# Signs and low halves of the converted weights on GpSimd in a chain of attention and two expert layers

## The chip, the cores and the metric

One core of one Trainium2 chip runs the whole program in one launch. The metric is the device time of one execution in microseconds; the median over the runs is given. An execution under the profiler gives the trace from which all rows come.

## The reference

Three stages follow one another:

```python
qn = q / (norm(q, axis=1) + 1e-6); kn = k / (norm(k, axis=1) + 1e-6)   # B, N, C = 2, 6016, 256
a = softmax(kn.transpose(0, 2, 1) @ qn / tau)      # 256 x 256 per batch
x = (v @ a).reshape(12032, 256)
h = x @ w_in;  x = (h - tanh(h)) @ w_out           # d_ff 2048
out = (sigmoid(x @ w_gate) * (x @ w_val)) @ w_out2 # d_ff 1536
```

The five weight matrices (w_in, w_out, w_gate, w_val, w_out2) are float64 arrays. They reach the kernel as pairs of 32-bit words and are turned into float32 on the core.

## The kernel before

**Tiling.** The tokens are cut into 24 blocks of 496 or 512 columns, 12 per batch, with the channels on the 128 partitions. Before the blocks the start-up loads q and k of batch 0 in chunks (`load_raw`), multiplies them on TensorE (`boot_s`, L570), squares them on ScalarE (L578) and sums the squares on VectorE into `accb` (L581). The 256x256 softmax (`s_softmax`) follows, and `aw_chunk` multiplies its result into w_in, so that v needs only one product in place of two.

**Steps.** Then one loop over T runs; a step of it handles one slice f of 128 of the 2048 hidden columns of a block: `emit_H` (TensorE, L332 and L334) makes h of slice T, `emit_E` (ScalarE L342 to L346, VectorE L347 to L350) makes h - tanh(h) of slice T - 1, `emit_gs` splits slice T - 2 into a high and a low half (ScalarE L355, VectorE L356), and `emit_X` (L378 to L381) multiplies it. `emit_GV`, `emit_S`, `emit_ps` and `emit_O` do the same for the gated layer, a block behind. Most products are made of three: high by high, high by low and low by high halves of the operands in the format fp32r, of which ScalarE writes the high half as a rounded copy and VectorE the low half as the difference.

**Converting a weight.** `conv` is a generator that runs once for each of 34 tiles of 128x512 elements: 8 of w_in, 8 of w_out, 18 of the gate, value and second output weights. It loads the word pairs (L125) into `st`. ScalarE scales the high words, read as float32, by 2^-112 into `bt` (L135): that puts the exponent right. A second ScalarE instruction (L136) overwrites the upper 16 bits of the high word by a half-precision zero that carries the sign, VectorE shifts the upper three bits of the low word into the lower 16 bits (L138), and a last VectorE instruction shifts `bt` left by three and ors that word in (L143). For the 18 tiles of the gated layer a further step makes the high half (L149) and the low half (L150). `split_w1` does the same for the 8 tiles of w_out (L184, L187).

**Order.** The schedule is written out by hand; each engine works through its own instructions in program order. In `at(step, ...)` a background generator is given a step at which it begins; the list `running` then advances each generator by one `yield None` per step T, after `emit_S` and before `emit_H`. `whole` passes over the `yield 1`, so that the whole conversion (L135 to L143) falls into one step. In start-up the generators `tail` are advanced piece by piece between the pieces of the softmax. The steps GV0 say when a pair of gate and value slices of block 0 is first multiplied; a conversion begins at least three steps before (`late`). The buffers of `st` are 4 in start-up (`boot4`) and 3 later (`v4`), those of `bt` 4 (`cv`). GpSimd holds only the constants, one fill of `accb` and the 46 sums of squares of batch 1 (L688), from 366 us on.

Of the kernel before, what the change touches and what calls it, by code (L numbers as in the profile page):

```python
# [8 lines left out]
F32 = mybir.dt.float32  # L9
F32R = mybir.dt.float32r  # L10
BF16 = mybir.dt.bfloat16
U32 = mybir.dt.uint32
U16 = mybir.dt.uint16
F16 = mybir.dt.float16
AF = mybir.ActivationFunctionType
ALU = mybir.AluOpType
AX = mybir.AxisListType
# [10 lines left out]
def kernel(  # L28
# [13 lines left out]
    nc = tc.nc  # L42
# [18 lines left out]
    rest, i = N - WB * nb, nb // 2  # L61
    assert 0 <= rest <= nb * (TB - WB)
    while rest:
        widths[i] += QB
        rest -= QB
        i = (i + 1) % nb
    blocks = []
    for b in range(B):
        t = 0
# [23 lines left out]
    def cv(name, shape=(P, 512)):  # L93
        return cv_p.tile(list(shape), F32, tag="cv", name=name)
# [22 lines left out]
    w1_hi = [wp.tile([P, 2, C], F32R, name=f"w1h{i}") for i in range(N1 // 2)]  # L117
    w1_lo = {}
    win_d = dr_p.tile([N1 // 2, P, NK, 2 * P], F32, name="win_d")

    def conv(src, shape, pool, tag, name, w=None, hi=None, lo=None):

        a, m = shape
        st = pool.tile([P, a, 2 * m], U32, tag=tag, name=f"st_{name}")
        nc.sync.dma_start(out=st, in_=src)  # L125
        yield
        words = st.rearrange("p a (m t) -> p a m t", t=2)
        low, high = words[:, :, :, 0], words[:, :, :, 1]
        half = st.bitcast(U16).rearrange("p a (m t) -> p a m t", t=4)
        bt = cv(f"cb_{name}", (P, a, m))  # L130
        bu = bt.bitcast(U32)

        nc.scalar.activation(bt, high.bitcast(F32), AF.Copy, scale=2.0**-112)  # L135
        nc.scalar.activation(half[:, :, :, 3].bitcast(F16), high.bitcast(F32), AF.Copy, scale=2.0**-96)  # L136
        yield 1
        nc.vector.tensor_scalar(half[:, :, :, 2], half[:, :, :, 1], 13, None, ALU.logical_shift_right)  # L138
        yield 1
        yield 1  # L140
        if callable(w):
            w = w()
        nc.vector.scalar_tensor_tensor(  # L143
            out=bu if w is None else w.bitcast(U32), in0=bu, scalar=3, in1=high,
            op0=ALU.logical_shift_left, op1=ALU.bitwise_or
        )
        if w is None:
            yield
            nc.scalar.activation(hi, bt, AF.Copy)  # L149
            nc.vector.tensor_tensor(out=lo, in0=bt, in1=hi.bitcast(F32), op=ALU.subtract)  # L150

    def whole(g):

# [7 lines left out]
    def conv_win(i, pool, tag="st"):  # L161
        src = words(w_in)[:, i * 512:(i + 1) * 512].rearrange("(k p) f -> p k f", p=P)
        yield from conv(src, (NK, 2 * P), pool, tag, f"wi{i}", w=win[i])
# [7 lines left out]
    w1_f = {}  # L171

    def conv_w1(i):
        src = words(w_out)[i * 256:(i + 1) * 256, :].rearrange("(a p) d -> p a d", p=P)

        def home():
            pool, tag = (wp, f"w1l{i - 4}") if i > 3 else (wp2, f"w2{'hl'[i % 2]}{4 + i // 2}")
            w1_f[i] = pool.tile([P, 2, C], F32, tag=tag, name=f"w1f{i}")
            return w1_f[i]

        return conv(src, (2, C), v4_p, "v4", f"w1{i}", w=home)

    def split_w1(i):
        nc.scalar.activation(w1_hi[i], w1_f[i], AF.Copy)  # L184
        yield
        w1_lo[i] = wp.tile([P, 2, C], F32R, tag=f"w1l{i}", name=f"w1l{i}")
        nc.vector.tensor_tensor(out=w1_lo[i], in0=w1_f[i], in1=w1_hi[i].bitcast(F32), op=ALU.subtract)  # L187


    kq = {}  # L190
# [469 lines left out]
    def conv_m2(i, which):  # L660
        if which == 2:
            src = words(w_out2)[i * 256:(i + 1) * 256, :].rearrange("(a p) d -> p a d", p=P)
            for x, nm in ((w2_hi, "w2h"), (w2_lo, "w2l")):
                x[i] = wp2.tile([P, 2, 2 * P], F32R, tag=f"{nm}{i}", name=f"{nm}{i}")
            h, lo = w2_hi[i], w2_lo[i]
        else:
            w = (w_gate, w_val)[which]
            src = words(w)[:, i * 512:(i + 1) * 512].rearrange("(k p) f -> p k f", p=P)
            h, lo = ((wg_hi[i], wg_lo[i]), (wv_hi[i], wv_lo[i]))[which]
        return conv(src, (2, 2 * P), v4_p, "v4", f"m{which}{i}", hi=h, lo=lo)  # L670
# [43 lines left out]
    for i in range(N1 // 2):  # L714
        at({6: 16, 2: 18, 7: 19, 3: 20, 4: 21, 5: 23, 0: 25, 1: 26}[i], split_w1, i)
# [5 lines left out]
    for n in range(3 * N2 // 2):  # L721
        i, w = divmod(n, 3)
# [3 lines left out]
    for j in range(NT):  # L726
        t = 54 + 2 * j
# [121 lines left out]
```

## Time and profile before

| what | value |
|---|---|
| median of 3 runs | 2211.52 us (2211.27 to 2211.89) |
| profiled execution | 2212.01 us, of which the span from first to last instruction 2210.2 us |
| TensorE busy | 2199.5 us |
| VectorE busy | 1772.7 us |
| ScalarE busy | 1602.0 us |
| GpSimd busy | 66.5 us |
| granted TensorE clock | 1.0 throughout |

PE is TensorE, PEld its weight loads, DVE VectorE, ACT ScalarE, POOL GpSimd. A row of the timeline gives start and length in us, the engine, the line of the kernel, and output <- inputs; a bracket at its end gives the idle time before it and what ended that. The length of an instruction is longer than its slot on a full engine, since the next one starts before the recorded end.

### The profile page before, as it was taken

To read this page: it belongs to the slowest core of one execution; us is meant where nothing else is said; L and a number is where in the kernel's file an instruction comes from. 1 tells how busy PE (TensorE), PEld (TensorE's weight loads), DVE (VectorE), ACT (ScalarE), POOL (GpSimd) and SP (SyncE) were. 2 spreads that over 40 slices of the span, in tenths; PEclk is the share of its full clock that TensorE was granted. 3 is DMA by queue.
4 is the path that set the end of the run, shared out by engine and by line. 5 is a ranking of instruction groups with operands and counts; after the bars stand their busy time and mean duration, and the time that the engine had idled before them with its cause. 6 is when DMAs were issued, how large, how long until landed. Compare 5 with 4: busy or idle time off the path is not lost.

```text
span 2210.2 us, 28820 instructions
## 1 busy us (share of the span) xinstructions
PE 2199.5 (100%) x10338; PEld 1944.1 (88%) x10338; DVE 1772.7 (80%) x2723; ACT 1602.0 (72%) x2811; POOL 66.5 (3%) x53
## 2 busy tenths in 40 slices
PE   9999999999999999999999999999999999999999
PEld 8778899898888888888999999999988888888898
DVE  7889877888888888878787787787787877877773
ACT  7988867777777777767677676776776776767763
POOL 0000000111111110000000000000000000000000
PEclk9999999999999999999999999999999999999999
DMA  9742101111111010001000000000000000000000
GB/s 354 241 147 96 38 1 53 34 29 52 35 29 48 27 36 20 1 24 34 19 19 1 19 19 1 19 19 1 19 20 1 19 20 1 20 1 19 10 1 19
DMA packets 54000, 86.54 MB, mean 39 GB/s; under 512 B 4960, under 2 KB 31072, under 8 KB 53856
## 3 DMA queue, kind: packets, MB, share of 16 engines
q1 hardware_dynamic: 53280, 83.91, 11.6%
q8 instruction: 81, 1.33, 0.3%
q10 hardware_dynamic: 576, 0.79, 0.1%
q14 instruction: 63, 0.52, 0.1%
HBM read 69.73 MB, written 14.94 MB: 38 GB/s over the span
## 4 chain that ended last, share of the span: by engine, by line
PE 93%; DVE 3%; ACT 3%; issue 1%; DMA 1%; ACTq 0%; DVEq 0%
PE o L445 16%; PE h L332 14%; PE h L334 7%; PE x L381 7%; PE x L378 7%; PE x L379 7%; PE va L414 5%; PE va L416 5%; PE va L413 5%; PE ga L414 5%; PE ga L413 5%; PE ga L416 5%; PE x L373 2%; PE kqe L517 1%; PE aw L285 1%
## 5 line engine op out<-in xcount | busy, mean ns | idle before, releaser
L347 DVE SCALAR_TENSOR_TENSOR w<-u,h 128x496 f32<-128x496 f32 (+1 forms) x384 | 259.6, 676 | 228.6 <-ACT t L343 227.7
L350 DVE COPY_PREDICATED w<-m,t 128x496 f32<-128x496 uint16 (+1 forms) x384 | 303.9, 792 | 39.9 <-ACT sr L687 0.5
L342 ACT ACTIVATE u<-h 128x496 f32<-128x496 f32 (+1 forms) x384 | 222.7, 580 | 138.8 <-PE h L334 138.3
L345 ACT ACTIVATE s<-u,cb 128x496 f32<-128x496 f32 (+1 forms) x384 | 273.8, 713 | 0.3 <-DVE w L349 0.3
L346 ACT ACTIVATE m<-u,ct 128x496 bf16<-128x496 f32 (+1 forms) x384 | 272.5, 710 | 0.0
L348 DVE TENSOR_TENSOR t<-h,t 128x496 f32<-128x496 f32 (+1 forms) x384 | 258.4, 673 | 0.0
L349 DVE SCALAR_TENSOR_TENSOR w<-s,w 128x496 f32<-128x496 f32 (+1 forms) x384 | 257.6, 671 | 0.0
L332 PE MATMUL h<-vTh,awh 128*128 128x496 f32 (+1 forms) x768 | 232.8, 385 | 0.0
L334 PE MATMUL h<-vTh,awl 128*128 128x496 f32 (+1 forms) x768 | 225.1, 375 | 0.2 <-DVE awl L291 0.2
L332 PE MATMUL h<-vTl,awh 128*128 128x496 f32 (+1 forms) x768 | 225.0, 375 | 0.0
L343 ACT ACTIVATE t<-h 128x496 f32<-128x496 f32 (+1 forms) x384 | 223.1, 581 | 0.0
L414 PE MATMUL va<-x2h,wvl 128*128 128x496 f32 (+1 forms) x552 | 206.9, 375 | 0.0
L414 PE MATMUL ga<-x2h,wgl 128*128 128x496 f32 (+1 forms) x552 | 206.9, 375 | 0.0
L413 PE MATMUL va<-x2h,wvh 128*128 128x496 f32 (+1 forms) x552 | 206.9, 375 | 0.0
L413 PE MATMUL ga<-x2h,wgh 128*128 128x496 f32 (+1 forms) x552 | 206.8, 375 | 0.0
L425 DVE TENSOR_TENSOR sg<-va,sg 128x496 f32<-128x496 f32 (+1 forms) x288 | 192.2, 667 | 18.1 <-PE va L416 18.1
L424 ACT ACTIVATE sg<-ga 128x496 f32<-128x496 f32 (+1 forms) x288 | 168.6, 585 | 11.2 <-PE ga L416 11.1
L416 PE MATMUL ga<-x2l,wgh 128*128 128x496 f32 (+1 forms) x576 | 168.8, 375 | 0.0
L416 PE MATMUL va<-x2l,wvh 128*128 128x496 f32 (+1 forms) x576 | 168.8, 375 | 0.0
L332 PEld LDWEIGHTS h<-vTh,awh 128*128 128x128 f32 x768 | 144.4, 189 | 24.5 <-issue 6.8
L334 PEld LDWEIGHTS h<-vTh,awl 128*128 128x128 f32 x768 | 145.1, 189 | 17.7 <-DVE awl L291 0.6
L332 PEld LDWEIGHTS h<-vTl,awh 128*128 128x128 f32 x768 | 145.1, 189 | 17.2
(358 smaller groups left out, 4425.8 us busy)
## 6 DMA issues: line engine op xcount, KB each, us to landing
v<-in_v_dram SPq DMA_DIRECT2D x16, 496.0 KB, 4.2
out_dram<-ob SPq DMA_DIRECT2D x15, 496.0 KB, 3.0
sr<-in_q_dram SPq DMA_DIRECT2D x47, 128.0 KB, 2.1
sr<-in_k_dram SPq DMA_DIRECT2D x47, 128.0 KB, 2.3
raw<-in_q_dram SPq DMA_DIRECT2D x13, 384.0 KB, 8.1
raw<-in_k_dram SPq DMA_DIRECT2D x12, 384.0 KB, 8.2
st_wi<-in_moe_w_in_dram SPq DMA_DIRECT2D x8, 512.0 KB, 7.0
st_w<-in_moe_w_out_dram SPq DMA_DIRECT2D x8, 512.0 KB, 4.7
```

What stands on the lines that cost most here:

```text
L332: MM(o[:, :n], aw_hi[i][:, kk, fs], turned(p, x[:, kk, :n]), start=x is h and kk == 0, stop=False)
L334: MM(o[:, :n], aw_lo[i][:, kk, fs], turned(p, h[:, kk, :n]), start=False, stop=kk == 1)
L345: nc.scalar.activation(s, u, AF.Square, bias=cb)
L346: nc.scalar.activation(m, u, AF.Relu, bias=ct2)
L347: nc.vector.scalar_tensor_tensor(out=w, in0=u, scalar=C2, in1=hp, op0=ALU.mult, op1=ALU.mult)
L348: nc.vector.tensor_tensor(out=t, in0=hp, in1=t, op=ALU.subtract)
L349: nc.vector.scalar_tensor_tensor(out=w, in0=s, scalar=CG, in1=w, op0=ALU.add, op1=ALU.mult)
L350: nc.vector.copy_predicated(w, m.bitcast(U16), t)
L413: MM(o[:, :n], wht[m // 2][:, d, ms], h[d], start=d == 0, stop=False)
L414: MM(o[:, :n], wlt[m // 2][:, d, ms], h[d], start=False, stop=False)
L416: MM(o[:, :n], wht[m // 2][:, d, ms], lo[d], start=False, stop=d == 1)
L445: MM(ops[p][d][:, :n], w[i][:, a, ds[d]], x, start=m == 0 and w is w2_hi and x is ph, stop=m == N2 - 1 and x is pl)
```

## The change

For each converted tile the second ScalarE instruction is left out. GpSimd compares the high word, read as float32, with zero and multiplies by -2^31; written as a 32-bit integer in place, that is the sign bit alone. VectorE shifts the low word right by 29 and ors the sign in, in place of the shift of 16-bit halves; the last shift and or then takes this word. The low halves of the 18 tiles of the gated layer and of the 8 tiles of w_out are subtracted on GpSimd instead of VectorE.

```diff
@@ conv
-        half = st.bitcast(U16).rearrange("p a (m t) -> p a m t", t=4)
...
         nc.scalar.activation(bt, high.bitcast(F32), AF.Copy, scale=2.0**-112)
-        nc.scalar.activation(half[:, :, :, 3].bitcast(F16), high.bitcast(F32), AF.Copy, scale=2.0**-96)
+        nc.gpsimd.tensor_scalar(high.bitcast(I32), high.bitcast(F32), 0.0, -2.0**31, ALU.is_lt, ALU.mult)
         yield 1
-        nc.vector.tensor_scalar(half[:, :, :, 2], half[:, :, :, 1], 13, None, ALU.logical_shift_right)
         yield 1
+        nc.vector.scalar_tensor_tensor(
+            out=low, in0=low, scalar=29, in1=high, op0=ALU.logical_shift_right, op1=ALU.bitwise_or
+        )
         yield 1
...
         nc.vector.scalar_tensor_tensor(
-            out=bu if w is None else w.bitcast(U32), in0=bu, scalar=3, in1=high,
+            out=bu if w is None else w.bitcast(U32), in0=bu, scalar=3, in1=low,
             op0=ALU.logical_shift_left, op1=ALU.bitwise_or
         )
         if w is None:
             yield
             nc.scalar.activation(hi, bt, AF.Copy)
-            nc.vector.tensor_tensor(out=lo, in0=bt, in1=hi.bitcast(F32), op=ALU.subtract)
+            nc.gpsimd.tensor_tensor(out=lo, in0=bt, in1=hi.bitcast(F32), op=ALU.subtract)
@@ split_w1
-        nc.vector.tensor_tensor(out=w1_lo[i], in0=w1_f[i], in1=w1_hi[i].bitcast(F32), op=ALU.subtract)
+        nc.gpsimd.tensor_tensor(out=w1_lo[i], in0=w1_f[i], in1=w1_hi[i].bitcast(F32), op=ALU.subtract)
```

## Rows read from the trace of the kernel before

**Rows 1.** The page's part 1: busy us, share of the span, instructions, by engine.

```profile
PE 2199.5 (100%) x10338; PEld 1944.1 (88%) x10338; DVE 1772.7 (80%) x2723; ACT 1602.0 (72%) x2811; POOL 66.5 (3%) x53
```

**Rows 2.** Busy time of each engine in stretches (the head row names the columns).

```profile
core 0: us, PE busy (x) PEld busy (x) DVE busy (x) ACT busy (x) POOL busy (x), PEclk, DMA share, GB/s
...
12.00:46.00 34.00, 33.35 (x155) 29.41 (x156) 32.23 (x27) 28.48 (x26) 0.00 (x0) 1.00 1.01 376
...
70.00:200.00 130.00, 130.00 (x536) 101.29 (x535) 115.05 (x182) 115.48 (x184) 0.00 (x0) 1.00 0.49 155
200.00:250.00 50.00, 47.94 (x223) 41.18 (x222) 48.10 (x78) 44.93 (x77) 0.00 (x0) 1.00 0.15 47
250.00:2210.00 1960.00, 1955.48 (x9283) 1745.07 (x9281) 1558.91 (x2400) 1388.30 (x2489) 64.44 (x46) 1.00 0.06 20
```

**Rows 3.** Waits of TensorE: who waited for whom, us, times, longest.

```profile
PE va L414 <- DVE wvl L150: 1.5, 1, 1.5
...
PE x L378 <- ACT g_14h L355: 0.6, 1, 0.6
```

**Rows 4.** Timeline of start-up: start, length (us), engine, line, operation.

```profile
45.11 0.63 ACT L578 ACTIVATE sq<-raw 128x512 f32<-128x512 f32 x1 [0.70 <-DVE accb L581]
...
46.58 1.35 ACT L136 ACTIVATE st_wi<-st_wi 128x512 f16<-128x512 f32 x1
...
47.94 1.28 ACT L637 ACT_TABLE_LOAD   x1
...
49.82 1.06 PE L203 MATMUL n<-ones,sq 128*128 128x64 f32 x8
...
50.97 1.35 ACT L136 ACTIVATE st_wi<-st_wi 128x512 f16<-128x512 f32 x1
...
52.07 0.25 ACT L214 ACTIVATE rn<-n 128x4 f32<-128x4 f32 x1
```

**Rows 5.** Timeline of VectorE in start-up, one converted tile.

```profile
21.80 0.74 DVE L138 TENSOR_SCALAR st_wi<-st_wi 128x512 uint16<-128x512 uint16 x1
22.57 0.69 DVE L143 SCALAR_TENSOR_TENSOR win<-cb_wi,st_wi 128x512 uint32<-128x512 uint32 x1
23.18 1.75 DVE L581 TENSOR_TENSOR accb<-accb,sq 128x1536 f32<-128x1536 f32 x1
```

**Rows 6.** Chain that ended last, 185 to 260 us: start, us, what.

```profile
214.61 1.36 ACT st_m L136
...
239.62 0.61 DVE wvl L150
```

**Rows 7.** GpSimd by line: count, busy us, mean ns, idle before.

```profile
L688 POOL TENSOR_TENSOR acc<-acc,sr 128x512 f32<-128x512 f32 x46 | 64.4, 1401 | 790.9 <-ACT sr L687 790.9
L546 POOL MEMSET accb<- 128x1536 f32 x1 | 1.4, 1383 | 0.0
masks.py:199 POOL TENSOR_SCALAR_AFFINE_SELECT ident<-ident 128x128 f32<-128x128 f32 x1 | 0.3, 294 | 0.0
```

**Rows 8.** Timeline around two adds on GpSimd and VectorE beside them.

```profile
377.65 1.27 POOL L688 TENSOR_TENSOR acc<-acc,sr 128x512 f32<-128x512 f32 x1 [10.26 <-ACT sr L687]
...
377.78 1.72 DVE L350 COPY_PREDICATED w<-m,t 128x496 f32<-128x496 uint16 x1
...
387.90 0.72 DVE L350 COPY_PREDICATED w<-m,t 128x496 f32<-128x496 uint16 x1
...
388.25 1.48 POOL L688 TENSOR_TENSOR acc<-acc,sr 128x512 f32<-128x512 f32 x1 [9.33 <-ACT sr L687]
...
389.31 0.95 DVE L356 TENSOR_TENSOR g_11l<-w,g_11h 128x496 fp32r<-128x496 f32 x1
...
390.18 0.66 DVE L356 TENSOR_TENSOR p_7l<-sg,p_7h 128x496 fp32r<-128x496 f32 x1
```

**Rows 9.** VectorE by line, the removed shift of 18 tiles.

```profile
L138 DVE TENSOR_SCALAR st_m<-st_m 128x512 uint16<-128x512 uint16 x18 | 13.5, 748 | 2.4 <-ACT st_m L136 2.4
```

**Rows 10.** Timeline of ScalarE, the last value weight's high half.

```profile
237.32 0.64 ACT L149 ACTIVATE wvh<-cb_m 128x512 fp32r<-128x512 f32 x1
```

More of the change, by code (lines that the diff above doesn't have):

```diff
@@ L13 @@
 U16 = mybir.dt.uint16
-F16 = mybir.dt.float16
+I32 = mybir.dt.int32
 AF = mybir.ActivationFunctionType
```

## The prediction

> **What bounds the kernel now.** I read the page's busy line first: TensorE is busy 2199.5 us of a span of 2210.2 us [rows 1]. The reader is to see that only 10.7 us are not TensorE's, and that no relief of another engine can give more than its part of these. Next I cut the span by stage [rows 2]: from 250 us to the end, where nothing of the change runs, TensorE works 1955.48 of 1960 us. Delay from before 250 us is therefore not won back, and a gain there stays. From 70 to 200 us TensorE never idles, although VectorE works 115.05 of 130 us beside it. From 200 to 250 us it idles 2.06 us, and there VectorE is full: 48.10 of 50 us. The view of waits names what ends TensorE's idle time [rows 3]: the low half of a value weight (1.5 us, once) and the high half of an activation (0.6, once); most of the others are in start-up, before 63 us. The page's own 2212.01 us of the profiled execution stands 0.5 us above the median of the runs, 2211.52; I sum against it and take 0.5 off at the end.
>
> **The change part by part.** Each of 34 converted tiles loses one ScalarE instruction (L136) and one VectorE instruction (L138); it gains one on GpSimd (the sign) and one on VectorE (shift and or), which waits for the sign. Behind it on VectorE stand the second shift and the low halves of the activations (L356), and TensorE waits for those. 26 low halves (18 on L150, 8 on L187) go from VectorE to GpSimd. No DMA is moved, no queue of SP gets another order.
>
> *ScalarE* loses 34 instructions of 1.35 us [rows 4]. In the steady part I cost that at nothing, since TensorE sets the pace there. In start-up two of them stand in line between the last squares (45.11) and the root of the norms (52.07): the instruction behind the first starts 1.36 us after it, the root 1.10 us after the second, so 2.46 us come out of that line [rows 4].
>
> *VectorE.* On a full VectorE L138 holds 0.77 us (21.80 to 22.57) and a two-input shift 0.61 us (22.57 to 23.18) [rows 5], so the exchange saves 0.16 us per tile. A low half holds 0.61 us [rows 6].
>
> *The sign on GpSimd* is not in the trace. GpSimd fills 1536 elements in 1.383 us, so 512 in 0.46 us with no input; its two-input add of 512 takes 1.27 us undisturbed [rows 7, 8]. In between stands the one-input select: 0.294 us for 128 elements, 1.18 us for 512 if all of it scales. I take 0.9 us and keep 0.46 and 1.27 as ends. One input at "roughly line-rate" is the price in the Trainium skill, GPSIMD Engine Reference, Engine selection: 512 elements at 1.2 GHz would be an estimated 0.43 us, no row here shows it, and with it start-up would come out 1.1 us early instead of level.
>
> *What a GpSimd instruction costs VectorE.* The rows of 377 us show it: the add starts at 377.65, the predicated copy 0.13 us later, and the copy takes 1.72 us in place of the 0.72 of the next pair, so it lost 1.00 us [rows 8]. In the other order (388 us) the add takes 1.48 us, 0.21 us more than 1.27, because the copy still ran, and the subtraction after it takes 0.95 instead of 0.66, a loss of 0.29 [rows 8]. Both orders alternate over the 46 adds. So an add of 1.27 us costs VectorE 0.64 us in the mean and 1.0 at worst; a sign of 0.9 us, in proportion, 0.45 and 0.71. Below zero it can't go, for GpSimd gives VectorE nothing.
>
> *Start-up, 12 to 46 us.* VectorE works 32.23 of 34 us [rows 2], mostly on two-input sums of squares, and GpSimd can get in only between them. It is let in about 0.17 us before the recorded end (the copy of 387.90 had 0.37 us to go, the add waited 0.21, rows 8), and the new shift waits for the sign: each of four tiles costs the sign less 0.17 and less 0.16, and with some 0.08 us to pass the signal on, 0.9 - 0.25 = 0.65 us. Four make 2.6 us, and ScalarE's squares hang on the sums. The root then comes at 52.07 - 2.46 + 2.6 = 52.2 us: +0.1. What waits behind it is the softmax, the first chunk of combined weights and the first h. With the ends: 0.46 gives 4 x 0.21 = 0.8, but the norm's matmuls end at 50.88 [rows 4], so no more than 1.1 us is to be had; 1.27 gives 4 x 1.02 = 4.1, so +1.6.
>
> *70 to 250 us.* By the starts of their lines all 26 low halves and 25 signs lie here (four signs lie before 46 us, five from 46 to 70 us). Saved: 26 x 0.61 + 25 x 0.16 = 19.9 us. Blocked: 26 x 0.64 + 25 x 0.45 = 27.9 us. VectorE gets 8.0 us more to do and had 130 - 115.05 + 50 - 48.10 = 16.9 us free [rows 2], so over the whole it still fits, and in front of 200 us it costs nothing. By length 2.2 us of the 8.0 fall between 200 and 250 us, where 1.9 are free and TensorE waits already. The 2.4 us that L138 waited for ScalarE on 18 of these tiles [rows 9] go, of which I put 0.8 in this stretch (the chain runs through such a wait at 214.61, rows 6); the sign is in the same place of the order, but 0.45 us shorter. I put the rest on the chain at about 1.0 us later.
>
> *The late value weight.* The subtraction that TensorE waits 1.5 us for starts at 239.62 [rows 6], behind other work of VectorE. Its high half is ready at about 238.0 (L149 starts at 237.32 and takes 0.64) [rows 10]; GpSimd could begin then, with VectorE busy on PSUM inputs, and be done at 239.3 instead of 240.2: 0.9 us won. If that cover is gone and it is blocked first, it costs the 0.6 us by which 1.27 exceeds 0.68.
>
> **Sum:** +0.1 + 0 + 1.0 - 0.9 = +0.2 us, 2212.2 for a profiled execution, 2211.7 as a median.
>
> **The rivals.**
> *GpSimd holds up VectorE (slower).* Place: the two-input instructions from 70 to 250 us. Every low half and sign meets one in the dear order: 26 x 1.0 + 25 x 0.71 = 43.8 us, less 19.9 saved, is 23.9 us, 7.0 more than is free. With start-up at +1.6 and the value weight 0.6 later that is +9.2: 2221. It decides from the point where the added time passes what is free in its stretch, and 200 to 250 us is near that point already. For it: the 1.72 us row, and that the copy and the second product have both inputs in SBUF in each of the steps. Against: half of the rows show only 0.29. The Trainium skill, SBUF — State Buffer, Who interferes with whom, has the stricter form: whoever comes second "fully blocks" until the other is done. By that rule with full lengths it would be 26 x 1.27 + 25 x 0.9 - 19.9 - 16.9 = 18.7 us and 2230; the trace agrees in kind and shows 1.00 of 1.27 at most.
>
> *The freed engines show (faster, but small).* The sign takes 0.5 us, start-up gives its 1.1 us, and the waits from 200 to 250 us vanish, 2.1 us: 2208.3. For it: every one of these waits has one of the removed or moved instructions in front of it. Against: VectorE is not relieved if its losses count. It stays within 0.2% of before, since there is hardly more idle time of TensorE to be had.
>
> *The change doesn't free VectorE where it matters:* the low half is 0.6 us longer on GpSimd and a sign waits behind it in the same queue, while the shift on VectorE waits for that sign, with all later work of the step behind it. At two or three tiles converted just before their use that is +1.2 to +1.8: 2213.
>
> **How the numbers follow.** A measurement of this kernel tells about 0.2% (4.4 us) from no change. My forecast, no change, 0.53 at 2211.7; the small gain 0.21; the longer low half 0.06; the blocked VectorE 0.20. Of the small gain 0.05 may pass 4.4 us if start-up gives more than I see. Faster 0.05, within 0.74, slower 0.21. The range runs from 2208.2, where all of the idle time in reach is used, to 2217.5, which takes in more than half of the way to the rival at 2221.
>
> **What would show it.** Right: GpSimd gets 34 + 26 instructions more, about 60 us; the predicated copies from 70 to 250 us grow past 0.8 us in the mean; VectorE's load there stays near before in spite of fewer instructions; the value weight's wait falls below 1 us; the root of the norms starts within 1 us of 52; from 250 us on nothing differs but a shift. Wrong: a sign of over 1.3 us, waits of TensorE between 70 and 200 us where there were none, or sums of squares that end after 50 us.

## The result and the profile after

The changed kernel takes 2239.34 us (median of four runs, 2238.14 to 2241.04). The kernel before, run beside it, takes 2211.70 us. The ratio is 1.0125, with a 95% interval of 1.0108 to 1.0143: slower by 27.6 us, where +0.2 us had been forecast and 2217.5 us was the upper end of the range. The profiled execution took 2238.28 us, 26.3 more than the profiled one before.

First the busy line, to be held against [rows 1].

```profile
PE 2206.1 (99%) x10338; PEld 1945.2 (87%) x10338; DVE 1778.8 (80%) x2697; ACT 1562.1 (70%) x2777; POOL 182.1 (8%) x113
```

TensorE has the same 10338 products and is only 6.6 us busier; 19.7 of the 26.3 us are idle time. ScalarE has 34 instructions and 39.9 us less to do and nothing came of it. VectorE has 26 instructions less and is 6.1 us *busier*. GpSimd has 60 instructions more, as forecast, but they take 115.6 us in place of the forecast 60.

Next the stretches, in the columns of [rows 2].

```profile
12.00:46.00 34.00, 33.77 (x157) 29.78 (x158) 25.10 (x20) 18.86 (x17) 13.34 (x4) 1.00 0.98 365
46.00:70.00 24.00, 17.96 (x77) 14.74 (x75) 17.32 (x30) 13.54 (x24) 8.32 (x4) 0.86 0.92 321
70.00:200.00 130.00, 125.79 (x505) 95.07 (x506) 111.37 (x155) 88.66 (x155) 63.59 (x35) 1.00 0.49 148
200.00:250.00 50.00, 43.09 (x191) 34.99 (x191) 43.50 (x56) 31.11 (x58) 23.30 (x14) 1.00 0.26 83
```

The reader is to see a contradiction: between 12 and 46 us, and again from 70 to 250 us, VectorE is less busy than before (25.10 for 32.23; 111.37 for 115.05; 43.50 for 48.10), and yet TensorE idles in these stretches or right behind them. An engine that does less and delivers later is waiting. A second reading places the loss: matching each product of TensorE with the same one before, the start is 4.5 us later at the norms' products (48.98 us before), 7.8 at the first h (62.39), 8.4 at 128, 13.8 at 177, 21.3 at 212 and 26.2 at 242 us. From there to the end it stays between 25.8 and 26.2.

The waits of TensorE, longest first (answering [rows 3]):

```profile
PE n L203 <- DVE accb L585: 4.6, 1, 4.6
PE x L381 <- DVE g_0l L356: 2.3, 3, 1.9
PE va L413 <- DVE sg L425: 2.2, 2, 1.1
PE x L373 <- DVE w L350: 2.1, 3, 0.9
...
PE x L378 <- ACT g_14h L355: 1.6, 1, 1.6
...
PE va L414 <- POOL wvl L150: 0.6, 1, 0.6
```

All but the last are new or grown. Most name VectorE's work, and the high halves that ScalarE makes (L355) read what VectorE's copy (L350) wrote. What VectorE itself waits for is GpSimd's sign. Here is GpSimd by line (columns as in [rows 7]); in the changed kernel the sign is L134, the shift with the sign L137, the last shift and or L143:

```profile
L134 POOL TENSOR_SCALAR st_m<-st_m 128x512 int32<-128x512 f32 x18 | 37.9, 2108 | 32.1 <-ACT cb_m L133 21.8 <-issue 10.3
L134 POOL TENSOR_SCALAR st_wi<-st_wi 128x512 int32<-128x512 f32 x8 | 22.0, 2754 | 48.9 <-ACT cb_wi L133 47.9 <-DMA er<-in_k_dram 1.0
...
L187 POOL TENSOR_TENSOR w1l<-w1f,w1h 128x512 fp32r<-128x512 f32 x8 | 13.7, 1716 | 0.0
```

A sign takes 2.0 us at the least and 2.75 in the mean for w_in. The view of the sign's line says who waited for it (us, times):

```profile
who waited for it (us, times):
  DVE st_m L137: 14.1, 12
  DVE st_wi L137: 9.2, 6
  DVE st_w L137: 6.4, 6
```

VectorE's L137 waited for it on 24 of 34 tiles, 29.7 us in all. (A twenty-fifth wait, of 1.91 us at 24.60, the profile puts down to a transfer that landed; the sign's own row shows that it ended then.)

Start-up, one tile on VectorE (start, length, engine, line; against [rows 5]), and the end of the sums:

```profile
17.21 5.48 DVE L581 TENSOR_TENSOR accb<-accb,sq 128x1536 f32<-128x1536 f32 x3
24.60 0.69 DVE L137 SCALAR_TENSOR_TENSOR st_wi<-st_wi 128x512 uint32<-128x512 uint32 x1 [1.91 <-DMA raw<-in_q_dram]
25.40 0.69 DVE L143 SCALAR_TENSOR_TENSOR win<-cb_wi,st_wi 128x512 uint32<-128x512 uint32 x1
26.01 5.48 DVE L581 TENSOR_TENSOR accb<-accb,sq 128x1536 f32<-128x1536 f32 x3
...
52.72 0.69 DVE L585 TENSOR_TENSOR accb<-accb 128x512 f32<-128x512 f32 x1
55.31 0.69 DVE L137 SCALAR_TENSOR_TENSOR st_wi<-st_wi 128x512 uint32<-128x512 uint32 x1 [1.90 <-POOL st_wi L134]
```

The signs of the same stretch on GpSimd, the second one and that of the first tile after the sums:

```profile
21.13 3.44 POOL L134 TENSOR_SCALAR st_wi<-st_wi 128x512 int32<-128x512 f32 x1 [5.36 <-ACT cb_wi L133]
...
53.25 2.03 POOL L134 TENSOR_SCALAR st_wi<-st_wi 128x512 int32<-128x512 f32 x1 [11.13 <-ACT cb_wi L133]
```

The sign of 21.13 us is let in only where the sums end (17.21 + 5.48 = 22.69), and VectorE then stands still for 1.91 us until it is done at 24.57. From one group of sums to the next it is 8.80 us, where it was 6.78 (16.40 to 23.18): 2.0 us per tile. L585, the last of the sums, starts at 52.72, where it was 45.91.

Later the sign also stands behind low halves. The timeline of GpSimd at 178 us:

```profile
177.93 1.60 POOL L150 TENSOR_TENSOR w2l<-cb_m,w2h 128x512 fp32r<-128x512 f32 x1 [3.39 <-ACT w2h L149]
179.50 1.71 POOL L187 TENSOR_TENSOR w1l<-w1f,w1h 128x512 fp32r<-128x512 f32 x1
181.18 1.99 POOL L134 TENSOR_SCALAR st_m<-st_m 128x512 int32<-128x512 f32 x1
```

VectorE at the same time:

```profile
178.50 1.61 DVE L350 COPY_PREDICATED w<-m,t 128x496 f32<-128x496 uint16 x1
...
183.20 0.69 DVE L137 SCALAR_TENSOR_TENSOR st_m<-st_m 128x512 uint32<-128x512 uint32 x1 [2.54 <-POOL st_m L134]
```

Both ways of losing stand in these rows: the copy, blocked by the low half, takes 1.61 in place of 0.72 us [rows 8], and L137 then waits 2.54 us for a sign that could begin only when two low halves were done.

### The profile page after: what moved, and what is told of

It reads as the page before. It is cut to its first block, busy times and chain, and to the rows that moved or that the text cites. A ratio compares the mean times of both kernels' runs of the same rounds, so it can differ in the third digit from the quotient of the medians.

```text
span 2236.5 us, 28926 instructions
## 1 busy us (share of the span) xinstructions
PE 2206.1 (99%) x10338; PEld 1945.2 (87%) x10338; DVE 1778.8 (80%) x2697; ACT 1562.1 (70%) x2777; POOL 182.1 (8%) x113
## 4 chain that ended last, share of the span: by engine, by line
PE 86%; DVE 6%; ACT 3%; POOL 2%; issue 2%; DMA 1%; ACTq 0%; DVEq 0%; SPq 0%; POOLq 0%
PE o L445 15%; PE h L332 13%; PE x L381 7%; PE h L334 6%; PE x L378 6%; PE x L379 6%; PE va L414 5%; PE ga L414 5%; PE va L416 5%; PE ga L413 5%; PE va L413 5%; PE ga L416 5%; DVE w L350 1%; DVE w L349 1%; POOL st_m L134 1%
## 5 line engine op out<-in xcount | busy, mean ns | idle before, releaser
L350 DVE COPY_PREDICATED w<-m,t 128x496 f32<-128x496 uint16 (+1 forms) x384 | 311.0, 810 | 40.9 <-DVE w L349 1.8
L349 DVE SCALAR_TENSOR_TENSOR w<-s,w 128x496 f32<-128x496 f32 (+1 forms) x384 | 270.2, 704 | 0.0
L332 PE MATMUL h<-vTh,awh 128*128 128x496 f32 (+1 forms) x768 | 233.3, 385 | 0.0
L332 PE MATMUL h<-vTl,awh 128*128 128x496 f32 (+1 forms) x768 | 225.2, 375 | 0.1
L332 PEld LDWEIGHTS h<-vTh,awh 128*128 128x128 f32 x768 | 144.1, 189 | 25.2 <-issue 7.2
L332 PEld LDWEIGHTS h<-vTl,awh 128*128 128x128 f32 x768 | 145.1, 189 | 17.6 <-DVE vTl L311 0.5
```

The lines of the kernel that those rows point to most:

```text
L332: MM(o[:, :n], aw_hi[i][:, kk, fs], turned(p, x[:, kk, :n]), start=x is h and kk == 0, stop=False)
L349: nc.vector.scalar_tensor_tensor(out=w, in0=s, scalar=CG, in1=w, op0=ALU.add, op1=ALU.mult)
L350: nc.vector.copy_predicated(w, m.bitcast(U16), t)
```

## Experiments

Two theories were held against each other. **L** (latency): VectorE works in order, waits at L137 for the sign, and all of its later work waits with it. **P** (port): GpSimd's instructions hold up VectorE's two-input instructions, whether or not anything is waited for. Each difference below is against the kernel before on the same chip (2211.56 to 2211.68 us).

**The sign alone, and the low halves alone.** `sign_only` puts both subtractions back on VectorE:

```diff
-            nc.gpsimd.tensor_tensor(out=lo, in0=bt, in1=hi.bitcast(F32), op=ALU.subtract)
+            nc.vector.tensor_tensor(out=lo, in0=bt, in1=hi.bitcast(F32), op=ALU.subtract)
```

(and the same for `w1_lo`). 

> The sign on GpSimd stays, the 26 low halves go back to VectorE. Theory L (the sign is long, 2.0 us undisturbed, and VectorE stands in its order until it is done): most of the 27.6 us stays, since start-up (+7.8 us at the first h) has no low half in it and each shift still waits for its sign; without a low half in front of it in GpSimd's queue a sign comes earlier, so 2226 to 2233 us. Theory P (GpSimd's instructions hold VectorE's two-input instructions up, in proportion to GpSimd's busy time, of which the signs are 78.5 and the low halves 37.1 of 115.6 us): 2211.7 + 0.68 x 27.6 = 2230 us. The two agree here; low_only and sign_unused tell them apart.

Measured: 2225.26 us, ratio 1.0062 [1.0045, 1.0078], +13.6 us. TensorE is 8.9 us late at the first h and 12.5 at 242 us. The figure is a little under the range. The signs do hold up VectorE's two-input instructions, but only a little. A sign of GpSimd and the copy beside it:

```profile
224.88 1.99 POOL L134 TENSOR_SCALAR st_m<-st_m 128x512 int32<-128x512 f32 x1 [10.21 <-DVE w L349]
...
224.95 1.14 DVE L350 COPY_PREDICATED w<-m,t 128x496 f32<-128x496 uint16 x1
```

The copy begins 0.07 us into the sign and takes 1.14 us in place of 0.72, a loss of 0.42. Copies that begin 0.24 us into a sign of this run (at 194.76, 212.68 and 243.23) lose 0.25, and one that begins 0.62 us into it (230.57) loses nothing.

`low_only` is the kernel before with these two lines on GpSimd and the sign as it was. 

> The 26 low halves on GpSimd, the sign as before (ScalarE and VectorE). Theory L: nobody but TensorE waits for a low half, and VectorE is spared 26 x 0.61 us; within 3 us of before, 2210 to 2215 us. Theory P: 0.32 x 27.6 = 9 us more, 2220 us.

Measured: 2215.73 us, 1.0019 [1.0009, 1.0028], +4.1 us: small, but clear of no change by its interval, and 0.7 us over L's range. Most of it, 3.5 us, is lost between 208 and 242 us. VectorE there:

```profile
206.33 1.66 DVE L138 TENSOR_SCALAR st_m<-st_m 128x512 uint16<-128x512 uint16 x1 [0.73 <-ACT st_m L136]
...
211.03 1.42 DVE L349 SCALAR_TENSOR_TENSOR w<-s,w 128x496 f32<-128x496 f32 x1
...
229.29 1.59 DVE L350 COPY_PREDICATED w<-m,t 128x496 f32<-128x496 uint16 x1
```

and GpSimd beside it:

```profile
206.11 1.27 POOL L187 TENSOR_TENSOR w1l<-w1f,w1h 128x512 fp32r<-128x512 f32 x1
210.64 1.28 POOL L150 TENSOR_TENSOR wvl<-cb_m,wvh 128x512 fp32r<-128x512 f32 x1 [3.26 <-ACT wvh L149]
...
228.66 1.65 POOL L150 TENSOR_TENSOR wgl<-cb_m,wgh 128x512 fp32r<-128x512 f32 x1 [4.99 <-DVE t L348]
```

Each low half starts ahead of VectorE's instruction. The shift L138, which has one input, takes 1.66 us in place of 0.75; the second product L349 takes 1.42 in place of 0.66; the copy loses 0.9 us. TensorE then waits 1.3 us for the high half of g_11 and 1.4 for that of g_14, where before it waited 0.6 for the second alone. So the port does cost something, where VectorE is full. At 200 us TensorE is only 0.4 us late, near the nothing that had been forecast up to there.

**The sign made, but not waited for.** `sign_unused` is `sign_only` with a shift that doesn't read GpSimd's result:

```diff
-        nc.vector.scalar_tensor_tensor(
-            out=low, in0=low, scalar=29, in1=high, op0=ALU.logical_shift_right, op1=ALU.bitwise_or
-        )
+        nc.vector.tensor_scalar(low, low, 29, None, ALU.logical_shift_right)
```

> The low halves on VectorE; the sign is made on GpSimd as after the change, but VectorE only shifts the low word and does not read the sign, so no weight has a sign in this kernel and nothing waits for GpSimd. Theory L: the wait is gone, the blocking of two-input instructions stays; start-up and the stretch to 250 us come back to within 5 us of before, 2209 to 2217 us. Theory P: as sign_only, 2226 us or more.

Measured: 2210.64 us, 0.9994 [0.9985, 1.0004], -1.0 us. GpSimd does all 34 signs and the 13.6 us are gone. TensorE is full again in the stretch where it had idled:

```profile
70.00:200.00 130.00, 130.00 (x536) 101.35 (x535) 114.72 (x181) 91.52 (x164) 43.26 (x20) 1.00 0.50 157
```

For the signs that speaks for L and against P. (The shift has one input here and two in the changed kernel; `sign_early` below keeps both.) The timeline of its start-up shows why. VectorE:

```profile
12.16 1.76 DVE L579 TENSOR_TENSOR accb<-accb,sq 128x1536 f32<-128x1536 f32 x1 [0.22 <-ACT sq L576]
13.84 0.87 DVE L137 TENSOR_SCALAR st_wi<-st_wi 128x512 uint32<-128x512 uint32 x1
14.82 0.71 DVE L141 SCALAR_TENSOR_TENSOR win<-cb_wi,st_wi 128x512 uint32<-128x512 uint32 x1
```

and GpSimd's sign:

```profile
12.78 3.03 POOL L134 TENSOR_SCALAR st_wi<-st_wi 128x512 int32<-128x512 f32 x1 [10.20 <-ACT cb_wi L133]
```

The sign is let in when the sum ends near 13.8 us and runs to 15.81. The two-input L141 (14.82 to 15.53) runs inside it at its usual 0.7 us.

**Why the sign takes 2 us.** `forms` is the kernel before, with a fill and five one-input instructions of 128x512 put on the idle GpSimd at the start: compare and multiply into integers, the same into f32, a multiplication into f32 and into integers, a comparison alone. 

> The kernel before, with five one-input instructions of 128x512 elements on GpSimd at the start, on tiles that are not in use yet: compare and multiply to int32 (the sign's form, unit step), the same to f32, multiply alone to f32, multiply alone to int32, compare alone to f32. If the conversion to int32 makes the sign long, the first and the fourth are near 2 us and the others near 1; if the two operations do, the first and second are long; if the step of two words of the real sign does, all are under 1.3 us. Whole kernel: 2211 to 2214 us.

Measured in a single execution (2210.96 us, no different from before):

```profile
3.12 1.93 POOL L551 TENSOR_SCALAR win<-win 128x512 int32<-128x512 f32 x1
5.12 1.92 POOL L552 TENSOR_SCALAR win<-win 128x512 f32<-128x512 f32 x1
7.13 1.50 POOL L553 TENSOR_SCALAR win<-win 128x512 f32<-128x512 f32 x1
8.71 1.49 POOL L554 TENSOR_SCALAR win<-win 128x512 int32<-128x512 f32 x1
10.28 1.64 POOL L555 TENSOR_SCALAR win<-win 128x512 f32<-128x512 f32 x1
```

The conversion to integers costs nothing (1.93 against 1.92, 1.49 against 1.50). One multiplication takes 1.5 us and the comparison ahead of it adds 0.4. (The comparison alone, 1.64, ran beside VectorE's first sums of squares from 9.87 us on and may be held up by them.) The starts say the same: 2.0 us from one to the next with two operations, 1.6 with one. The sign is long because a one-input instruction of this length is long on GpSimd, not because of its format; its step of two words, which no form here has, adds 0.1 us at most (1.99 to 2.03 against 1.93).

**Is it the length that counts?** `after_short` is the changed kernel with a sign of one operation, a multiplication by 0; it writes 0 for every sign, so all weights come out positive:

```diff
-        nc.gpsimd.tensor_scalar(high.bitcast(I32), high.bitcast(F32), 0.0, -2.0**31, ALU.is_lt, ALU.mult)
+        nc.gpsimd.tensor_scalar(high.bitcast(I32), high.bitcast(F32), 0.0, None, ALU.mult)
```

> The whole change, but GpSimd only multiplies by zero into the integers (one operation, no compare), so the weights have no sign in this kernel; everything that waits for the sign still waits. One operation took 1.50 us in the run with the forms and the sign's two 1.93. If the sign's length is what counts, four in start-up and some 20 waits of VectorE later get 0.45 us shorter each: 5 to 9 us less than the change, 2230 to 2234 us. If the number of GpSimd's instructions counts and not their length, 2237 to 2240 us.

Measured: 2229.35 us, 1.0080 [1.0066, 1.0094], +17.8, which is 9.9 us less than the changed kernel's loss and a little more than the range had. The sign of the gated layer's tiles falls from 2.11 to 1.68 us in the mean, and TensorE's wait for the sums from 4.6 to 3.1. So 0.43 us of each sign is worth some 10 us over 34 of them, 0.3 us each: most of a sign's length goes straight into the time.

**The first tiles against the late ones.** `late_old` makes the sign on GpSimd for the first six tiles of w_in alone, as before for the other 28; all low halves are on GpSimd:

```diff
+        old = not (name[:2] == "wi" and int(name[2:]) < 6)
...
+        if old:
+            nc.scalar.activation(half[:, :, :, 3].bitcast(F16), high.bitcast(F32), AF.Copy, scale=2.0**-96)
+        else:
+            nc.gpsimd.tensor_scalar(high.bitcast(I32), high.bitcast(F32), 0.0, -2.0**31, ALU.is_lt, ALU.mult)
```

> The sign on GpSimd for the first six tiles of w_in alone, the other 28 as before; all low halves on GpSimd. Start-up should lose what it lost in sign_only (7.9 us at the first product behind the softmax) and the stretch to 250 us what it lost in low_only (3.9): 2222 to 2225 us. If start-up's loss is won back later, 2216 to 2219 us.

Measured: 2223.36 us, 1.0052 [1.0038, 1.0066], +11.7, as expected. Less the 4.1 of the low halves, the six signs of start-up cost 7.6 us; the trace of the changed kernel shows 7.8 at the first h.

**TensorE's clock.** After its wait of 4.6 us the granted clock of the changed kernel falls. Stretches of 5 us:

```profile
50.00:55.00 5.00, 1.53 (x7) 1.53 (x8) 3.17 (x4) 3.81 (x7) 1.75 (x1) 0.82 1.06 400
55.00:60.00 5.00, 5.00 (x18) 4.41 (x18) 4.04 (x8) 3.24 (x7) 2.63 (x2) 0.50 1.04 337
```

The granted 0.50 is the lower of the two levels, 1.2 GHz, after a stretch in which TensorE worked 1.53 of 5 us; the norms' two groups of products take 1.97 and 1.92 us in place of 1.00 and 1.06. `after_warm` fills the wait with products that nobody reads:

```diff
+                warm(20, "warm1")
                 nrm[0] = psw("n0", ...)
```

> The whole change; 20 more 128x128 products of ones are put ahead of the norms' products on TensorE, to fill the 4.6 us in which it waits for the sums of squares. After that wait the granted clock was 0.50 from 55 to 60 us, and the loss grew from 4.5 us at the first product of the norms to 7.5 us at 59.6. If that is the clock's doing, the clock stays at 1.0 and 2.5 to 3 us come back, 2235.5 to 2237 us; if the products behind the wait were late for another reason, 2238 to 2241 us.

Measured: 2238.40 us, 1.0121 [1.0107, 1.0135], not told from the changed kernel, and outside the range that the clock had been given: a miss. The timeline of its TensorE:

```profile
54.04 1.03 PE L203 MATMUL n<-ones,accb 128*128 128x64 f32 x8
...
59.86 0.78 PE L236 MATMUL rq<-dg,ones 128*128 128x128 f32 x4 [2.11 <-DVE dg L223]
60.43 4.39 PE L517 MATMUL kqe<-er 128*128 128x256 f32 x12
```

The norms' products are at full clock, but the 1.8 us that they give back are waited again, 2.11 us for `dg`. VectorE is late there because a further conversion stands in front of it (the sign of 53.25 us in the fence above). But the fill did not keep the clock up; it moved its fall behind the next wait:

```profile
60.00:65.00 5.00, 5.00 (x20) 4.19 (x20) 4.04 (x13) 2.04 (x6) 0.00 (x0) 0.66 0.95 313
```

The twelve products of 60.43 take 4.39 us, where they took 2.76 in the changed kernel and before. Counted from L585, the last of the sums, `rq` starts 0.9 us earlier than in the changed kernel, the first products of h (L332) 0.7 us later, and the one that waits for `awl` (62.39 before) within 0.1 us of it. So this run doesn't separate the clock from the wait: no run has the start-up wait without the lower clock. By the `rq` of the two kernels the lower clock costs some 0.9 us on the way there; it is not shown to cost more, nor to be free.

**The sign one step earlier.** In `sign_early` the shift follows the sign by one step of the loop, conversions begin one step earlier, and in start-up the tail's shifts stand behind the softmax. `after_early` is the same with the low halves on GpSimd:

```diff
         nc.gpsimd.tensor_scalar(high.bitcast(I32), ...)
-        yield 1
+        yield
...
-        late = GV0[2 * i] - 3 + (w == 2)
+        late = GV0[2 * i] - 4 + (w == 2)
```

> As sign_only (low halves on VectorE), but the sign is issued one step before the shift that reads it, and in start-up the two shifts of the last tiles stand behind the softmax; the conversions of the gated layer that begin just in time begin one step earlier. Same instructions, only the order differs. Theory L (waiting in order for a long sign): the 13.6 us of sign_only go, 2209.5 to 2213 us. Theory P (holding up two-input instructions): the port is used as much as in sign_only, 2220 us or more.

> The whole change, with the sign one step early as in sign_early. Theory L with the queue (in GpSimd's order a sign stands behind the low halves, and that is where 27.6 - 13.6 - 4.1 = 9.9 us come from): what low_only costs is left, 2213 to 2218 us. Theory P: 2228 us or more.

Measured: `sign_early` 2215.43 us, 1.0020 [1.0011, 1.0029], +3.8, some 2 us over its range. `after_early` 2216.27 us, 1.0021 [1.0011, 1.0030], +4.6, inside L's range and far from P's. With every instruction of the change still in place, 23.1 of the 27.6 us are gone. L137 waits once, 0.8 us at 60.06, where it waited on 24 tiles; at the first h TensorE is 0.2 us late instead of 7.8. (The kernel before was not run with this order, so what the order alone would give it isn't shown. The traced execution is the longest of ten, 2219.02 us.) VectorE is still blocked as before: its two-input instructions between 75 and 275 us are 21.0 us longer in sum, against 24.4 in the changed kernel. What is left shows in this trace as waits of TensorE for weights that now come late:

```profile
PE x L373 <- DVE w1f L143: 2.5, 1, 2.5
...
PE h L334 <- DVE awl L291: 1.5, 1, 1.5
```

`sign_early2` and `after_early2` move the conversions of w_out against these: the first two 2 steps later, the others one step earlier.

```diff
-        at(2 * i - (1 if i > 1 else 3), lambda i=i: whole(conv_w1(i)) if i > 1 else w1_first[i])
+        at(2 * i - (2 if i > 1 else 1), lambda i=i: whole(conv_w1(i)) if i > 1 else w1_first[i])
```

> As sign_early, with the conversions of w_out moved as well: the first two begin two steps later, behind the first low half of the combined weights (TensorE waited 1.5 us for that one), the others one step earlier (TensorE waited 1.5 us for the last converted tile). If these two waits are what is left of the loss, 2211 to 2213 us; if it is blocking, 2215 us as before.

> The whole change with the same order as sign_early2. After_early lost 4.6 us, of which 1.5 and 2.5 in the same two waits: 2211.5 to 2214 us, within 0.15% of the kernel before. If the low halves' blocking counts as in low_only, 2215 to 2217 us.

Measured: 2215.96 us, 1.0020 [1.0011, 1.0029], and 2218.09 us, 1.0031 [1.0020, 1.0042]. Both missed: the wait for `w1f` went and others came (for `awl` 1.7 us, for w 1.0 and 1.5). The first figure lies where blocking had been put, so what the last 3.8 to 4.6 us are, late weights or blocking, stays open. No version with all the signs was found that beats the kernel before.

**Sign before low half in the queue.** The parts add up to 4.1 + 13.6 = 17.7 us, the whole is 27.6. `after_swap` tests whether the other 9.9 us are the place of a sign behind low halves in GpSimd's queue: the background generators are advanced youngest first, so a step's sign is issued ahead of its low halves.

```diff
-        running = [g for g in running if next(g, running) is None]
+        running = [g for g in running[::-1] if next(g, running) is None][::-1]
```

> The whole change; in each step the background generators are advanced youngest first, so that a sign no longer stands behind a low half of the same step in GpSimd's order. Nothing begins earlier. If the 9.9 us by which the change costs more than its two parts come from that queue, most of them go: 2228 to 2232 us. If they come from blocking of VectorE by both kinds, 2236 us or more.

Measured: 2235.80 us, 1.0108 [1.0095, 1.0122], only 3.4 us less loss, which the intervals don't tell from none: a miss, and 0.2 us under what blocking by both kinds had been given. The waits of L137 between 75 and 275 us fall from 19.7 to 10.3 us, but L137 itself is now blocked (GpSimd and VectorE at 175 us):

```profile
175.54 1.29 POOL L187 TENSOR_TENSOR w1l<-w1f,w1h 128x512 fp32r<-128x512 f32 x1
...
175.64 1.75 DVE L137 SCALAR_TENSOR_TENSOR st_m<-st_m 128x512 uint32<-128x512 uint32 x1 [2.00 <-POOL st_m L134]
```

Freed by the sign, it starts just after the low half that stood behind the sign and takes 1.75 us in place of 0.69: 12.2 us longer in sum over the stretch. So the queue is only one way in which signs and low halves disturb one another. How the 9.9 us split (the intervals of the three ratios leave it uncertain by about 6) stays open; that an earlier sign removes them is shown, for `after_early` costs no more than `sign_early` and `low_only` do together.

## Why the prediction was wrong

**Right.** The bound and the method held: TensorE sets the time, what is lost before 250 us is kept, and no relief of ScalarE shows. The low half blocks as [rows 8] said: 26 x 0.64 = 16.6 us were forecast, and VectorE's instructions from 75 to 275 us grew by 17.9 us in `low_only`. The sum of all blocking was forecast as 27.9 us and is 24.4, but not by its parts: 25 signs were to cost 11.3 of it, and in `sign_only` VectorE's two-input instructions of that stretch grew by some 4 to 5 us in all. The late value weight's wait fell from 1.5 to 0.6 us, the 0.9 forecast. The Trainium skill, SBUF — State Buffer, Who interferes with whom, says that the later of the two "fully blocks": for the low halves the rows come near it (0.9 of 1.27 us). For the signs they don't: the copy of 224.95 us in `sign_only` lost 0.42 us behind a sign of 1.99.

**The step that failed: the sign on GpSimd, taken as 0.9 us with the ends 0.46 and 1.27.** It is 2.0 us, outside both ends. The fault lies in the upper end: the two-input add was taken as dearer than any one-input instruction, and `forms` shows 1.5 to 1.9 us against 1.27. The select of [rows 7], scaled to 1.18 us, was too cheap a neighbour. The Trainium skill, GPSIMD Engine Reference, Engine selection, has one input at "roughly line-rate", 0.43 us estimated; the shortest one-input instruction of this length took 1.49 us here, more than three times that.

With 2.0 us the prediction's own formula for start-up would have given 4 x (2.0 - 0.25) - 2.46 = +4.5. The norms' products do start 4.5 us late (48.98 to 53.47), but by other terms: the last sum starts 6.8 us late (0.8 for the first tile and 2.0 for each of three), and 2.3 us of that passed while TensorE, before as after, still had other products to make. The tile costs 2.0 and not 1.75, in part because the 0.16 us saved by the exchange don't exist: L143 follows L137 after 0.80 us, as it followed L138 after 0.77 [rows 5]. The 0.61 taken for a two-input shift was the slot of one whose successor doesn't need its result. The 0.08 allowed for the signal had no row; here it is 0.03 (24.57 to 24.60). The rest to 7.8 is the conversion behind the sums: its L137 waits for the sign of 53.25, the work on the root of the norms (from L218 on) stands behind it on VectorE, and the sum had not charged it. Some 0.9 us of it is the lower clock, by the `rq` of `after_warm`, and 1.1 us come in at the first h itself, where `awl` stands on VectorE behind a wait of 2.3 us for the sign of a w_out tile. With that shift moved behind the softmax, in `sign_early`, the products after the root start 1.1 us *earlier* than before.

**The step that hid it: 70 to 250 us, "in front of 200 us it costs nothing".** It set VectorE's added work against its free time and left the wait out. A wait is no work: VectorE became less busy (111.37 of 130 us) and TensorE idled 4.2 us all the same, because L137 stands ahead of the activations' low halves in VectorE's order. The load of an engine can't bound what an in-order wait costs. The 0.45 us that the sign had for being "in the same place of the order, but shorter" than ScalarE's instruction turned round: 2.0 against 1.35 us, and behind low halves more. From the first h to 242 us TensorE lost 18.4 us, where +0.1 had been forecast.

**The rivals.** The third one came nearest to the mechanism (a sign queued behind a low half, VectorE waiting in order with all later work behind it) and priced it for two or three tiles at 2213, with a chance of 0.06. The wait was right, but it came on 24 tiles, and most of it without a low half: in `sign_only`, with none on GpSimd, L137 still waited on 21 tiles, 20.7 us in all. The first one had slower at 2221 for the wrong reason: for the signs `sign_unused` and `sign_early` refute blocking, for the low halves `low_only` shows it at 4.1 us. All three of the signs named as proof against the forecast appeared: a sign over 1.3 us, waits of TensorE between 70 and 200 us, sums of squares that end after 50 us (53.4).

| cause | us | shown by |
|---|---|---|
| six signs of start-up waited for | 7.6 | `late_old` less `low_only` |
| later signs waited for | 6.0 | `sign_only` less 7.6 |
| low halves block VectorE | 4.1 | `low_only` |
| both kinds together | 9.9 | the remainder; gone with an earlier sign, else not split |

The line between the first two rows is uncertain by 1 to 2 us: in `sign_only`'s own trace it runs at 8.9 and 3.7. The first row includes what the lower clock costs, which no run separates.

## What to carry to other kernels

When work moves to another engine, price the wait of the consumer before its load: ask what stands behind the waiting instruction in its engine's order, and count the producer's full length there, not what the consumer has free. Issue the producer early: here the order alone took back 23 of 27.6 us. And where the trace has no row for an operation, bound it from above by something that is certainly dearer; a two-input add is not.

## What the hardware showed that was not expected

- On GpSimd 512 elements with one input take longer than with two: 1.50 us for a multiplication, 1.93 for a comparison and a multiplication, against 1.27 for a two-input subtraction.
- Integer output is free there (1.49 against 1.50 us).
- A one-input instruction of GpSimd waits for VectorE's two-input instructions (3.44 us recorded for a sign of 2.0), but then holds them up only at its beginning: in `sign_only` 0.42 us for a copy that starts 0.07 us into it, 0.25 at 0.24 us, nothing at 0.62 us; a two-input subtraction of 1.27 us holds a copy up by 0.9 to 1.0 us.
- Such a subtraction also held up a one-input shift of 16-bit words, 1.66 us in place of 0.75 (`low_only`, 206.33 us).
- One wait of 4.6 us was followed by a stretch at half of TensorE's clock (0.50), in which the norms' products took 1.8 us longer. Filled with products, that wait left the clock at 1.00, and the next one, of 2.1 us, brought it down instead (0.66 from 60 to 65 us, a mean of both levels).
